# Splitting a scratch write and a broadcast load by their outermost dimension of four

## Chip, cores, metric

One core of a Trainium2 chip. The metric is the time of one execution on the device, in microseconds (us). One run of the kernel before, 1818.09 us, was slow and is in no ratio. The rounds ran on more than one chip, and every ratio is to the kernel before in the same rounds.

## The reference, cut to what matters

```python
# x: (1, 512, 512, 96) bf16; dw: 3x3x96; w1: 96x384; w2: 384x96
out = depthwise_conv3x3(x, dw)
h = layernorm(out)                       # over the 96 channels
h = gelu(h @ w1)
gx = sqrt((h * h).sum(over all pixels) + 1e-6)
nx = gx / (gx.mean(-1) + 1e-6)
return x + (grn_gamma * (h * nx) + grn_beta + h) @ w2
```

`nx` needs a sum over all pixels, so the kernel passes twice over the image. Phase 1 makes the convolution, the norm, the first matmul and the sums. Phase 2 applies `w2`, with `h` either read back ("stored" blocks) or computed again from the normed values `yn` ("recompute" blocks). A block is four image rows; there are 128, and of each ten, three are stored and seven recomputed.

## The kernel before

The convolution leaves y on 128 partitions, partition = 32 x image row (r, 0 to 3) + channel group (c, 0 to 31), with three channels (i) by 512 pixels along the free dimension. The first matmul wants channels on the partitions, so `yn` goes through DRAM: a write, then a read in another shape. The reciprocal deviations (`r_dram`) are broadcast from DRAM to the 32 partitions of each row.

```python
def yn_dst(q):                                   # DRAM side of the write
    return yn_dram[q].rearrange("(c i) (r w) -> r c i w", i=NI, r=GR)     # GR = 4
# ... cut ...
def stage_bcast(k):                              # once for four blocks
    b0, n = BATCHES[k]
    rbc = rbcpool.tile([128, BATCH, W], bf16, name="rbc")
    sp.dma_start(out=rbc[:, :n, :].rearrange("p n w -> p (n w)"),
                 in_=bass.AP(r_dram[b0].tensor, r_dram[b0].offset,
                             [[n * W, GR], [0, 32], [1, n * W]]))         # four rows outermost
# ... cut ...
def stage_write(b):                              # once for each block
    sp.dma_start(out=yn_dst(b), in_=yns.pop(b)[:])
def stage_read(b):
    sp.dma_start(out=yn_ring[b % NYT][:C], in_=yn_src(b))                 # ynT
```

The loop is software-pipelined: a step runs the convolution of block s, the normalization (POOL) of an earlier block, the write and read of blocks between, and the first matmul of block s - 14. In this loop every transfer is issued by one engine, SP.

## Time and profile before

1797.85 us, median of 3 runs (1796.64 to 1807.63). From the profiled execution:

| | phase 1 (400 to 800 us) | phase 2 (1250 to 1795 us) |
|---|---|---|
| PE, ACT, DVE, POOL busy | 84%, 76%, 74%, 75% | 94%, 89%, 51%, 88% |
| mean DMA share | 0.61 | 0.98 |

First the page's strips, 40 slices of the span: the busy tenths of PE, and the mean busy tenths of the 16 DMA engines. The change of phases is the dip near slice 28.

```profile
PE   5588888887888889878888888656999999999998
...
DMA  3455656666565656665666565553999999999996
```

Then the windows view: busy us of each engine (and instructions), the granted clock, the DMA share and GB/s.

```profile
core 0: us, PE busy (x) PEld busy (x) DVE busy (x) ACT busy (x) POOL busy (x), PEclk, DMA share, GB/s
...
400.00:800.00 400.00, 336.38 (x7317) 188.61 (x7378) 295.75 (x486) 302.21 (x304) 301.18 (x224) 0.95 0.61 207
...
1250.00:1795.00 545.00, 511.38 (x7169) 375.62 (x7166) 276.78 (x510) 485.96 (x351) 482.17 (x286) 0.96 0.98 348
```

Phase 2 is full of DMA. Phase 1 shows nothing full, which by itself says only that an average hides the limit. The waits view (who waited for whom: us in total, times, longest) shows DMA behind several engines, first of all behind SP:

```profile
SPq L32 <- DMA yn_dram<-yn: 363.7, 97, 5.7
...
SPq L32 <- DMA r_dram<-rt: 78.2, 35, 3.8
...
SPq L32 <- DVE rt L32: 44.6, 17, 13.4
...
```

```profile
POOL yn L32 <- DMA rbc<-r_dram: 212.6, 31, 14.1
...
PE U L32 <- DMA ynT<-yn_dram: 82.7, 32, 10.1
...
PE Y L32 <- DVE y_bf L32: 35.4, 12, 5.6
```

The chain of work that ended last, from 100 to 1130 us, by line:

```profile
by line: DMA ynT<-yn_dram 14.9%; PE U L32 10.3%; DMA r_dram<-rt 9.4%; DVE bst L32 8.6%; DMA yn_dram<-yn 8.4%; PE Y L32 8.0%; SPq L32 4.8%; issue 4.4%; PE SG L32 4.3%; ACT gm L32 3.8%; ACT gt L32 3.7%; DVE xT L32 3.0%; another core or an unk
```

The DMA view has the number of transfers and the size of each:

```profile
yn_dram<-yn SPq DMA_DIRECT2D x128, 384.0 KB
...
rbc<-r_dram SPq DMA_DIRECT2D x31, 512.0 KB
```

What no view shows is how the 16 DMA engines share the load. The trace has a start and a length for every packet, so I counted the packets in flight at each moment from 100 to 1100 us. The count is of the queue that carries the kernel's own transfers; the fetches of instructions, which have a queue of their own, are left out here and in every such count below (with them, exactly four is 28% and five 17%):

```
packets in flight    0 to 3    exactly 4    5       6 to 14    15 and more
share of the time    0.02      0.36         0.10    0.16       0.36
```

The records don't name the engine of a packet. I read a lasting state of exactly four as four engines at work while the others have nothing to do; e3, e4 and e10 below test this reading.

### The profile page before, as it was taken

The page shows a single profiled execution, that of the slowest core. Times are in us where ns is not written, and L with a number is a line of the kernel's source. Part 1 is how long each engine was busy: PE and PEld are TensorE (multiplying, and loading weights), DVE is VectorE, ACT ScalarE, POOL GpSimd, SP SyncE. Part 2 cuts the span into 40 slices and gives each one's busy share as a digit, 9 for nine tenths or more (in the row PEclk, how much of TensorE's full clock was granted, in tenths as well). Part 3 has the DMA queues.
Part 4 walks back from the last instruction along what each step waited for, and adds up shares of the span by engine and source line. Part 5 has one row for each costly group of instructions (what it writes and reads, how often), then busy time and mean ns, then how long its engine had stood idle before and what let it go on. Part 6 is the DMA issues. An engine that isn't in the chain of part 4 may idle for free.

```text
span 1795.2 us, 63594 instructions
## 1 busy us (share of the span) xinstructions
PE 1508.7 (84%) x28145; PEld 926.2 (52%) x28302; DVE 1147.9 (64%) x1989; ACT 1371.8 (76%) x1236; POOL 1359.9 (76%) x972
## 2 busy tenths in 40 slices
PE   5588888887888889878888888656999999999998
PEld 2254444444444445444444444423667666666666
DVE  4256877777768677867786767656545554455455
ACT  2357777776777678767776778766989898889898
POOL 5678876787678767866787677532999998889896
PEclk9698999999999999999998989887999999999999
DMA  3455656666565656665666565553999999999996
GB/s 95 120 171 175 219 197 210 205 219 210 200 221 201 212 196 221 204 203 200 216 206 207 196 207 178 195 204 115 361 357 367 365 362 337 351 347 367 353 372 261
DMA packets 171879, 430.92 MB, mean 240 GB/s; under 512 B 27796, under 2 KB 77300, under 8 KB 171604
## 3 DMA queue, kind: packets, MB, share of 16 engines
q1 hardware_dynamic: 154212, 357.11, 58.2%
q0 software_dynamic: 15568, 69.74, 11.0%
q8 instruction: 222, 3.64, 0.8%
q14 instruction: 53, 0.43, 0.1%
q10 hardware_dynamic: 1824, 0.00, 0.1%
HBM read 267.41 MB, written 159.38 MB: 238 GB/s over the span
## 4 chain that ended last, share of the span: by engine, by line
DMA 37%; PE 32%; DVE 10%; ACT 9%; issue 4%; POOL 4%; SPq 4%; another core or an unknown queue 2%; ACTq 0%; DVEq 0%; POOLq 0%
PE U L32 15%; DMA ynT<-yn_dram 10%; DMA out_dram<-o_sb 10%; PE O L32 9%; DMA yn_dram<-yn 6%; DMA r_dram<-rt 6%; DVE bst L32 6%; PE Y L32 5%; SPq L32 3%; PE SG L32 3%; ACT gm L32 3%; ACT gt L32 2%; DVE xT L32 2%; ACT gth L32 2%; DMA gl<-g_dram 2%
## 5 line engine op out<-in xcount | busy, mean ns | idle before, releaser
L32 POOL TENSOR_TENSOR yn<-y_bf,rbc 128x1536 bf16<-128x1536 bf16 x128 | 396.5, 3097 | 245.4 <-DMA rbc<-r_dram 212.6
L32 ACT ACTIVATE gl<-U 128x1536 bf16<-128x1536 f32 x356 | 493.1, 1451 | 63.5 <-PE U L32 50.9
L32 DVE TENSOR_TENSOR o_sb<-O,xb 128x384 bf16<-128x384 f32 x512 | 277.8, 556 | 268.3 <-PE O L32 202.6
L32 DVE BATCH_NORM_STATS2 bst<-gth 128x6 f32<-128x512 bf16 x534 | 332.0, 672 | 172.6 <-ACT gth L32 172.6
L32 PE MATMUL Y<-xT,Wd 32*32 32x511 bf16 (+1 forms) x13374 | 359.6, 406 | 85.1 <-DVE y_bf L32 35.4
L678 POOL TENSOR_TENSOR xb<-xr,B2c 128x1536 f32<-128x1536 bf16 x128 | 400.5, 3130 | 26.8 <-DVE o_sb L32 17.6
L32 ACT ACTIVATE gth<-U 128x1024 bf16<-128x1024 f32 x267 | 263.6, 1026 | 203.1 <-issue 141.9
L32 POOL TENSOR_TENSOR ysq<-y_bf 128x1536 bf16<-128x1536 bf16 x128 | 351.6, 2747 | 47.2 <-ACT y_bf L32 23.7
L32 PE MATMUL U<-ynT,w1p 128*128 128x512 bf16 x845 | 285.7, 411 | 120.9 <-DMA ynT<-yn_dram 82.7
L32 PEld LDWEIGHTS <-gl 128*128 128x128 bf16 x6048 | 305.5, 99 | 120.0 <-issue 39.6
L32 DVE BATCH_NORM_STATS2 bst<-gt 128x6 f32<-128x512 bf16 x444 | 269.3, 676 | 128.7 <-ACT gt L32 128.4
L32 PE MATMUL O<-W2s,gl 128*128 128x96 bf16 x6048 | 326.5, 209 | 29.6 <-DVE o_sb L32 28.4
L32 PEld LDWEIGHTS <-w1p 96*128 96x128 bf16 (+1 forms) x2070 | 167.9, 100 | 326.3 <-issue 155.1
L32 PE MATMUL U<-ynl,w1p 96*128 96x512 bf16 x1068 | 300.8, 391 | 7.9 <-DVE junk L32 7.5
L32 PEld LDWEIGHTS <-Wd 32*32 32x32 bf16 x13806 | 165.5, 90 | 271.2 <-issue 212.7
L32 ACT ACTIVATE gt<-U 128x1024 bf16<-128x1024 f32 x222 | 215.4, 1033 | 71.6 <-remote 60.2
L32 ACT ACTIVATE gm<-U 128x1024 bf16<-128x1024 f32 x267 | 263.8, 1033 | 5.0 <-PE U L32 4.8
L32 ACT ACTIVATE y_bf<-Y 128x1536 bf16<-128x1536 f32 x102 | 148.6, 1456 | 45.7 <-PE Y L32 45.6
L32 DVE STREAM_TRANSPOSE xT<-xin 128x576 f32<-128x576 f32 (+1 forms) x256 | 181.0, 747 | 2.3 <-DMA xin<-in_x_dram 2.3
L32 PE MATMUL U<-w1p,ynT 128*128 128x384 bf16 (+2 forms) x1068 | 159.1, 283 | 12.2 <-ACT gth L32 4.2
L32 PEld LDWEIGHTS <-ynT 128*128 128x128 bf16 x1068 | 91.4, 101 | 99.8 <-issue 70.0
L32 PE MATMUL SG<-gm 128*128 128x128 bf16 x2136 | 136.2, 220 | 3.8 <-issue 3.7
(77 smaller groups left out, 731.7 us busy)
## 6 DMA issues: line engine op xcount, KB each, us to landing
g_dram<-gt SPq DMA_DIRECT2D x111, 512.0 KB
xin<-in_x_dram SPq DMA_DIRECT2D x126, 432.0 KB
yn_dram<-yn SPq DMA_DIRECT2D x128, 384.0 KB
ynT<-yn_dram SPq DMA_DIRECT2D x128, 384.0 KB
xr<-in_x_dram POOLq DMA_DIRECT2D x128, 384.0 KB, 7.7
out_dram<-o_sb SPq DMA_DIRECT2D x128, 384.0 KB
gl<-g_dram SPq DMA_DIRECT2D x74, 512.0 KB
ynl<-yn_dram SPq DMA_DIRECT2D x89, 384.0 KB
```

The costliest lines, as they stand in the source:

```text
L32: r = f(*a, **k)
L678: nc.gpsimd.tensor_tensor(out=xb[:], in0=grp[q]["xr"][:], in1=B2c[:, None, :].to_broadcast([128, PXP, C]), op=ALU.add)
```

## The change

The intent is that the outermost dimension of both kinds of transfer is 32 or more, so that each can use all 16 DMA engines.

```diff
-    def yn_dst(q):
-        return yn_dram[q].rearrange("(c i) (r w) -> r c i w", i=NI, r=GR)
+    def yn_dst(q, r):
+        return yn_dram[q].rearrange("(c i) (r w) -> r c i w", i=NI, r=GR)[r]
@@ stage_bcast
-            sp.dma_start(out=rbc[:, :n, :].rearrange("p n w -> p (n w)"),
-                         in_=bass.AP(r_dram[b0].tensor, r_dram[b0].offset, [[n * W, GR], [0, 32], [1, n * W]]))
+            for j in range(GR):
+                sp.dma_start(out=rbc[32 * j:32 * j + 32, :n, :].rearrange("p n w -> p (n w)"),
+                             in_=bass.AP(r_dram[b0].tensor, r_dram[b0].offset + j * n * W, [[0, 32], [1, n * W]]))
@@ stage_write
-            sp.dma_start(out=yn_dst(b), in_=yns.pop(b)[:])
+            yn = yns.pop(b)
+            for r in range(GR):
+                sp.dma_start(out=yn_dst(b, r), in_=yn[32 * r:32 * r + 32, :, :])
```

## The prediction

> **What bounds the kernel now.** Phase 1 (convolution, norm, first matmul) runs to about 1215 us, phase 2 after it. In the windows view, phase 2 (1250 to 1795 us) has the DMA share at 0.98; the change does not touch it. In phase 1 (400 to 800 us) no engine is full: PE 84%, ACT 76%, DVE 74%, POOL 75%, mean DMA share 0.61. The mean hides the limit. I counted packets in flight from the trace's packet records: from 100 to 1100 us exactly four were in flight in 36% of the time, fewer in only 2%. Four engines never rest while twelve often do. The 1,024-byte packets (yn writes) took 2,001 us in that 1,000 us window: 50% of each of four engines. The rbc broadcasts (26 batches of 128 packets of 4 KB, mean 197 ns) add about 16%, everything else, spread over sixteen, about 43%. The sum passes 100%: four engines are full, and phase 1 goes at their pace. The Trainium skill, "DMA: Bandwidth & Descriptors", section "Why a DMA increments its semaphore by 16 and not by 1", says a transfer uses the largest number of engines up to 16 that divides the outermost dimension of both sides: 4 for the yn write and the broadcast. The four in flight agree.
>
> **How it reaches the time.** In the waits view SP waits 364 us for yn writes (97 times), POOL 213 us for rbc, PE 83 us for ynT. In the chain, from 100 to 1130 us, ynT reads have 14.9%, r_dram 9.4%, yn writes 8.4%.
>
> **What the change does.** Bytes, packets and compute stay; the instruction order on PE, ACT, DVE and POOL is the same. yn writes and broadcasts have 32 outermost (96 on the write's DRAM side), so 16 engines each. The load becomes about 60% on all sixteen. Added: 384 + 102 issues on SP, 0.31 to 0.54 us each in the trace: about 1.7 us per step, SP then issuing 3 to 4 us of a step of 8. The issue order shows eight completion semaphores in turn, so a DMA waits for the one eight before it; with nine issues a step that is mostly the previous step's. The broadcast's last parts now wait for a g store and an x load just issued: a few us of SP once in four steps, with two steps of slack behind it. I expect none of this on the critical path.
>
> **Size.** A phase-1 step takes 8.83 us on average (first convolution matmul to the next). Undisturbed steps (lower quartile) are 6.8, 8.0 and 7.9 us by kind (recompute after stored, recompute after recompute, stored after recompute); weighted 0.3/0.4/0.3 that is 7.6, PE without a gap. ACT, DVE and POOL would each be near 90% then, so I allow 0.25 us of hiccups: 7.85. 121 steps times 1.0 us is 120 us, plus about 10 in the ramp, where the first ynT read takes 11 us. Phase 2: unchanged.
>
> Predicted: 1667 us, range 1630 to 1720 (8 in 10). Faster by over 2%: 0.94; within 2%: 0.05; slower by over 2%: 0.01.
>
> **What would show it.** Phase 1's DMA share rising to about 0.67, the four-in-flight plateau gone; SP's wait for yn writes and POOL's for rbc under 60 us each; PE in phase 1 at 93% or more; ynT and r_dram nearly gone from phase 1's chain; phase 2 as long as before (within 1%).
>
> **What would make it wrong.** Steps stay at 8.4 us or more since SP, with its in-order waits on eight semaphores, becomes the limit; DVE and ACT in stored steps lag more than undisturbed steps show; a 32-partition transfer is slower per packet; the granted clock drops as PE fills.

## More of the kernel before

One more part matters later, the copy of y out of PSUM (`y_bf`). PSUM holds one Y, so the next step's convolution waits for this copy:

```python
# per step, in the order of issue on the vector engine (DVE):
squares(...)                    # 12 statistics instructions in a stored step, 6 in a recompute step
turn_x(s + 2)                   # two transposes
evac(pm_rows(b) > 0 and s % 4 == 0)   # True: copy y on DVE, else on ACT; pm_rows > 0: recompute step
```

## The result, and the profile after

1730.42 us, median of 4 runs (1723.24 to 1740.58), against 1800.76 us (4 runs) for the kernel before in the same rounds. The ratio is 0.961, 95% interval 0.9549 to 0.9671. A ratio here is the mean time of one kernel's fast runs over that of the other's of the same rounds, so not quite the ratio of the medians. The gain is clear. It is about half of the predicted one, and the time lies above the predicted range.

The same lines after. Strips, then windows:

```profile
PE   5688888889888989898988998659989899999998
...
DMA  3458557766786578667857766767999999999995
```

```profile
400.00:800.00 400.00, 346.41 (x7542) 193.69 (x7600) 309.62 (x509) 311.44 (x313) 306.17 (x233) 0.95 0.71 219
...
1180.00:1731.00 551.00, 509.24 (x7172) 373.01 (x7170) 276.61 (x512) 485.86 (x351) 483.47 (x286) 0.97 0.97 344
```

The DMA share rose to 0.71, but PE is at 346.41 of 400 us, 87%. Waits of SP, then of the others:

```profile
SPq L32 <- DVE rt L32: 284.9, 33, 14.6
...
SPq L32 <- DMA yn_dram<-yn: 9.7, 9, 2.9
...
SPq L32 <- DMA r_dram<-rt: 1.0, 3, 0.4
```

```profile
PE Y L32 <- DVE y_bf L32: 35.7, 12, 5.6
...
PE Y L32 <- issue: 20.4, 23, 2.1
POOL yn L32 <- DMA rbc<-r_dram: 18.2, 7, 6.3
```

SP now waits for the transposed deviations, that is for the compute engines: it runs ahead of them. PE's wait for ynT is nearly gone:

```profile
PE U L32 <- DMA ynT<-yn_dram: 1.3, 1, 1.3
```

What did not move at all is PE's wait for the copy of y: 12 times, 35.7 us. The chain from 100 to 1070 us, and the transfers:

```profile
by line: PE Y L32 16.4%; PE U L32 16.2%; DVE bst L32 13.4%; PE SG L32 9.6%; issue 9.0%; ACT gm L32 6.8%; ACT gt L32 5.7%; another core or an unknown queue 4.4%; ACT y_bf L32 4.3%; ACT gth L32 3.9%; DVE xT L32 3.6%; DVE y_bf L32 1.9%; DVE mv
```

```profile
yn_dram<-yn SPq DMA_DIRECT2D x512, 96.0 KB
...
rbc<-r_dram SPq DMA_DIRECT2D x124, 128.0 KB
```

No transfer is left in the visible part of phase 1's chain. Exactly four packets were in flight in 0.7% of the time, none in 22%, 15 and more in 52%.

Where the 64 us between the two profiled executions went, from the start times in the traces:

| stretch | before | after | difference |
|---|---|---|---|
| start to first matmul U | 78.6 | 75.0 | -3.6 |
| to the last copy of y (the convolution loop) | 1039.0 | 996.1 | -42.9 |
| to the last U of phase 1 (pipeline drain) | 112.5 | 89.8 | -22.7 |
| the rest, phase 2 with it | 565.1 | 570.3 | +5.2 |

The +5.2 is no effect of the change: a second profile of the changed kernel (e12 below) has 556.7 there. That profile has 983.9 in the loop, so single profiles of one kernel differ by 12 to 14 us in such a stretch.

Setting the steps of the two traces side by side shows what changed and what didn't. Step = from the first convolution matmul to the next step's, in us; the numbering starts at the first convolution after the first statistics matmuls. The columns e2 and e5 are experiments below.

```
step    before   after   e2      e5
 32     15.50    9.00    8.51    8.50      <- waits for ynT in before
 52     12.57    8.51    8.50    8.52
 72     14.84    8.51    8.50    8.50
 92     13.74    8.81    8.51    8.50
112     15.53    8.86    8.51    8.37
 18      9.26    9.26    9.26    6.82      <- a DVE copy right behind a stored step
 26      9.61    9.60    9.61    6.81
 46     12.23   12.25   12.24    6.82
 58     11.89   12.24   11.67    6.84
 66      9.61    9.61    9.60    6.82
```

The first group, five of the steps that waited for ynT in before, lost its DMA waits. The second shows five of eleven such steps, which are within 0.4 us of each other with and without the change; the other six differ by up to 1.0, and all eleven sum to 108.7 us before and 107.4 after.

### The profile page after: what moved, and what is told of

It is laid out like the page before. It is cut to its first block, busy times and chain, and to the rows that moved or that the text cites. A ratio compares the mean times of both kernels' runs of the same rounds, so it can differ in the third digit from the quotient of the medians.

```text
span 1731.2 us, 64436 instructions
## 1 busy us (share of the span) xinstructions
PE 1494.7 (86%) x28145; PEld 919.5 (53%) x28302; DVE 1147.0 (66%) x1989; ACT 1370.4 (79%) x1236; POOL 1362.1 (79%) x972
## 4 chain that ended last, share of the span: by engine, by line
PE 43%; ACT 15%; DMA 15%; DVE 14%; issue 6%; another core or an unknown queue 3%; POOL 2%; SPq 1%; ACTq 0%; DVEq 0%; POOLq 0%
PE U L32 18%; DMA out_dram<-o_sb 11%; PE Y L32 10%; PE O L32 9%; DVE bst L32 9%; PE SG L32 6%; ACT gm L32 5%; ACT gt L32 4%; ACT gth L32 3%; ACT y_bf L32 3%; DVE xT L32 2%; DMA gl<-g_dram 2%; SPq L32 1%; DVE y_bf L32 1%
## 5 line engine op out<-in xcount | busy, mean ns | idle before, releaser
L32 PE MATMUL Y<-xT,Wd 32*32 32x511 bf16 (+1 forms) x13374 | 365.4, 405 | 100.9 <-DVE y_bf L32 35.7
L32 POOL TENSOR_TENSOR yn<-y_bf,rbc 128x1536 bf16<-128x1536 bf16 x128 | 397.0, 3102 | 24.5 <-DMA rbc<-r_dram 18.2
L32 PE MATMUL U<-ynT,w1p 128*128 128x512 bf16 x845 | 275.7, 397 | 41.3 <-ACT gm L32 12.9
L32 PE MATMUL U<-w1p,ynT 128*128 128x384 bf16 (+2 forms) x1068 | 153.5, 275 | 16.0 <-ACT gth L32 6.3
```

The source lines that it names most:

```text
L32: r = f(*a, **k)
```

## The experiments

Twelve more runs were made, eleven kernels and a repeat, all of them with correct results. The first question was whether four full DMA engines were the cause; the second, where the rest of the forecast gain is.

**e1: only the yn writes split.** The broadcast stays as it was.

```diff
-            for j in range(GR):
-                sp.dma_start(out=rbc[32 * j:32 * j + 32, ...   # the four parts
+            sp.dma_start(out=rbc[:, :n, :] ...                 # one transfer, as before
```

> Only the yn writes are split; the broadcast stays one transfer on four engines. Theory A (four full engines were the limit of phase 1): by the loads counted in the trace of before, the four engines carry about 12% (yn spread over sixteen) + 16% (rbc on four) + 43% = 71%, no longer full, so nearly the whole gain of the full change appears: ratio to before 0.960 to 0.970, and POOL's wait for rbc falls below 60 us though the broadcast is untouched. Rival B (POOL's 213 us wait for rbc, the longest wait at a compute engine, was the limit by itself): little gain here, ratio 0.99 or more, and POOL still waits for rbc.

Measured: 1719.87 us, ratio 0.9561 (0.9512 to 0.9611). The whole gain, even a little more than expected. But POOL's wait for rbc did not fall below 60 us:

```profile
POOL yn L32 <- DMA rbc<-r_dram: 102.2, 25, 10.4
```

So that detail of the expectation was wrong, and the wait is largely harmless: POOL waits 102 us for rbc in a kernel as fast as the full change. The largest wait of a compute engine in before was no measure of what removing it would give.

**e2: only the broadcasts split.** The yn writes stay one transfer with r = 4 outermost.

> Only the broadcasts are split; the yn writes stay on four engines. Theory A: the four engines still carry 50% + 4% + 43% = 97% and stay the limit: ratio 0.985 to 1.0, exactly four packets in flight still in over 20% of phase 1, SP still waits 200 us or more for yn writes. Rival B (the broadcast was the limit): ratio 0.960 to 0.970.

Measured: 1725.5 us, ratio 0.9558 (0.9498 to 0.9618). This is again the whole gain, and theory A as written (0.985 to 1.0) missed. Its other two expectations held: exactly four in flight in 20.5% of the time, and SP still waits for the writes.

```profile
SPq L32 <- DMA yn_dram<-yn: 332.9, 95, 5.7
```

Rival B gets its number here, but e1 had already shown that the broadcast can be left alone. What failed is my sum of loads. Before added up to 109%, which can't be: an engine has more than one packet in flight at times (in before, 17 and more were in flight on 16 engines in 12% of the time). If 109% stands for "full at 8.83 us a step", then 97% stands for 97/109 x 8.83 = 7.9 us, less than the 8.2 to 8.4 us that a step takes in e2 and in after. This was worked out after the fact; e8 below was to test it. In the time, either half of the change gives the whole gain.

**e3: the write in three transfers by i.** More and smaller transfers, all still with r = 4 outermost.

```diff
-            sp.dma_start(out=yn_dst(b), in_=yns.pop(b)[:])
+            yn = yns.pop(b)
+            for i in range(NI):
+                sp.dma_start(out=yn_dst(b)[:, :, i, :], in_=yn[:, i, :])
```

> The yn write is split into three transfers by i, each with r = 4 outermost and all 128 partitions: more and smaller transfers, but still four engines. Theory A: as before, ratio 0.99 to 1.015, four in flight still in a third of phase 1. Rival C (the gain came from smaller transfers, which are more of them in flight and land earlier, not from more engines): most of the gain, ratio 0.96 to 0.975.

Measured: 1797.73 us, ratio 0.9976 (0.9932 to 1.0019), exactly four in flight in 37% of the time. Rival C is out: splitting as such gives nothing. A trap is in this run's waits. SP's wait for the writes fell too, and the time didn't:

```profile
SPq L32 <- DMA yn_dram<-yn: 58.9, 74, 4.4
```

```profile
PE U L32 <- DMA ynT<-yn_dram: 71.1, 25, 10.1
```

**e4: the write in two transfers, two rows each.** Now two is outermost.

```diff
+            for r in range(0, GR, 2):
+                sp.dma_start(out=yn_dst(b)[r:r + 2], in_=yn[32 * r:32 * r + 64, :, :])
```

> The yn write as two transfers of two rows each, so two is outermost; broadcast as before. Theory A: two engines carry 100% (yn) + 16% + 43% = about 1.6 of the time that before needs for it, against 1.09 in before, so phase 1 (1,130 us) grows by about 46%: about 2,300 us in all, and the packet records show two in flight for over half of phase 1. Rival C (more transfers in flight is what helps): no slower than before.

Measured: 2307.76 us, ratio 1.281 (2 runs; 1.2734 to 1.2886), with exactly two packets in flight in 41% of the time and three in 11% (expected: two in over half). The forecast of 2,300 put two engines in place of four into the same sum of loads that e2 shows to be off, so its closeness is partly luck (phase 1 to its last U grew by a factor of 1.41, not 1.46). The direction and the plateau at two are not luck: with e3, they show that the number of engines counts, and not the number of transfers:

```profile
PE U L32 <- DMA ynT<-yn_dram: 531.1, 124, 13.3
```

The Trainium skill, "DMA: Bandwidth & Descriptors", section "Why a DMA increments its semaphore by 16 and not by 1", gives the rule by which the outermost dimension sets the number of engines; the counts here (four in flight for four, two for two, no plateau for 32) agree.

**e5: the full change, with the vector engine's copies of y moved.** In 11 steps the DVE copy comes right behind a stored step, whose twelve statistics instructions are still queued on DVE. This part of the timeline of the changed kernel shows one: start us, length, and in brackets the idle time before and what ended it.

```profile
537.68 0.44 PE L32 MATMUL SG<-rowsel,ysq 128*128 128x4 bf16 x12
543.69 1.50 PE L32 MATMUL Y<-xT,Wd 32*32 32x512 bf16 x36 [5.57 <-DVE y_bf L32]
```

```profile
530.85 4.80 DVE L32 BATCH_NORM_STATS2 bst<-gt 128x6 f32<-128x512 bf16 x8
535.58 2.76 DVE L32 BATCH_NORM_AGGREGATE mv<-bst 128x2 f32<-128x192 f32 x3
538.26 1.22 DVE L32 BATCH_NORM_STATS2 bst<-gth 128x6 f32<-128x512 bf16 x2
539.39 1.42 DVE L32 STREAM_TRANSPOSE xT<-xin 128x576 f32<-128x576 f32 x2
540.74 1.24 DVE L32 BATCH_NORM_STATS2 bst<-gth 128x6 f32<-128x512 bf16 x2
541.90 1.74 DVE L32 CAST y_bf<-Y 128x1536 bf16<-128x1536 f32 x1
```

PE is idle for 5.57 us until the copy (CAST) at 541.90 is done, and the copy stands behind 11 us of other work, nearly all statistics, with no gap on DVE. The next burst of 36 convolution matmuls takes 1.50 us; a burst elsewhere in this trace takes 0.89. The records of the granted clock have 0.5 from 542.4 us on, for 6.8 us. The Trainium skill, "TensorE: Matmul & The Clock Gate", section "Why this matters for your kernels", warns that idle gaps of PE above about 3 us bring the half clock; this gap of 5.57 us did. (This step, number 58, is one of the two slowest of the eleven.)

```diff
-                    evac(pm_rows(b) > 0 and s % 4 == 0)
+                    evac(pm_rows(b) > 0 and pm_rows(b - 1) > 0 and s % 2 == 0)
```

> The full change, and the copies of y out of PSUM that run on the vector engine are moved to recompute steps that follow a recompute step (about as many, 23 for 22). In before and in the changed kernel the same 11 steps, those with such a copy right behind a stored step, take 9.3 to 12.3 us, since the copy stands behind twelve statistics instructions and PE waits for it (36 us, 12 times, in all traces so far). Theory D (what the forecast counted as DMA trouble is this compute wait, which the change cannot touch): PE's wait for the copy falls below 10 us, and the time falls 25 to 50 us below the changed kernel's: ratio to before 0.935 to 0.948. Rival E (the copy's wait is slack that another engine takes over, the loop is limited by the engines' sum): ratio 0.955 or more.

Measured: 1692.09 us, ratio 0.9388 (0.9346 to 0.9431). PE's wait for DVE's copy is all but gone:

```profile
PE Y L32 <- DVE y_bf L32: 0.4, 1, 0.4
```

All eleven steps of that kind are at 6.8 us (column e5 above), and theory D holds. (The recorded 9.3 to 12.3 us is too narrow: in after the eleven steps take 8.5 to 12.3.) Over the eleven steps alone the traces of after and e5 differ by 32 us.

**e6: all copies on ACT.**

```diff
+                    evac(False)
```

> The full change, and all copies of y out of PSUM on ACT. Theory D: PE's wait for DVE's copy is gone altogether; ACT gets 22 x 1.3 us = 29 us more work and stays under 95%, so ratio to before 0.935 to 0.955. Rival E: ratio 0.96 or more.

Measured: 1699.81 us, ratio 0.9445 (0.9402 to 0.9488), as theory D expected.

**e7: the same move of the copies in the kernel before.**

> The kernel before, with the same move of the copies and no split. Theory A and D together: four full engines still set phase 1's pace, so the 36 us that PE no longer waits for the copy come back as waits for ynT: ratio 0.985 to 1.0. If the two losses are separate and simply add, ratio 0.975 to 0.98.

Measured: 1800.04 us, ratio 1.0004 (0.9961 to 1.0047). The same edit that gives 1.7 to 2.2% behind the change gives nothing without it. PE no longer waits for the copy and waits for ynT instead, 112.6 us in place of 82.7:

```profile
PE U L32 <- DMA ynT<-yn_dram: 112.6, 42, 10.3
```

**e8: only the broadcasts split, and the copies moved.**

> Only the broadcasts split, with the same move of the copies. The four engines' load is 97% of what 109% cost before: about 7.9 us a step, under the changed kernel's 8.4 but about what e5 should need. Theory A and D: the four engines come back as a limit, ratio 0.942 to 0.955, at most 0.01 above e5. If four engines no longer matter once the broadcast is split: the same as e5 within 0.004.

Measured: 1700.08 us, ratio 0.9441 (0.9403 to 0.9478). The interval overlaps that of e5, so whether the four engines cost anything here is not decided by the time. The trace leans to yes: exactly four in flight in 21.5% of the time, and PE waits 27.5 us for ynT, against 4.2 us in e5.

**e9: only the writes split, and the copies moved.**

> Only the yn writes split, broadcast on four engines, copies of y moved as in e5. The four engines carry 71% of what is 109% at the pace of before, so they are no limit at 7.9 us a step either: ratio to before 0.930 to 0.945, the same as e5 within 0.008, with 102 fewer transfers.

Measured: 1690.75 us, ratio 0.9366 (0.9329 to 0.9403): as e5, without the 102 extra transfers.

**e10: no split, another layout of the scratch tensor.**

```diff
-    yn_dram = dram.tile([NBLK, C, GR * W], bf16, name="yn_dram")
+    yn_dram = dram.tile([NBLK, 128, NI * W], bf16, name="yn_dram")
-        return yn_dram[q].rearrange("c (r w) -> c r w", r=GR)
+        return yn_dram[q].rearrange("(r c) (i w) -> (c i) r w", r=GR, i=NI)
-        return yn_dram[q].rearrange("(c i) (r w) -> r c i w", i=NI, r=GR)
+        return yn_dram[q]
```

> No split at all: the scratch tensor in DRAM is laid out as the yn tile lies in on-chip memory (128 rows of 3 KB), so one yn write has 128 outermost and 16 engines; reads of it then come as 1 KB packets in place of 4 KB. Broadcast on four engines, copies of y moved as in e5. If the number of engines is what counts, and not the number of transfers: as e9, plus at most 15 us in phase 2 for the smaller packets of the re-reads (89 x 384 packets of 47 ns against 89 x 96 of 159 to 197 ns, over 16 engines): ratio 0.930 to 0.955. If splitting as such is needed: 0.98 or more.

Measured: 1744.25 us, ratio 0.965 (0.9611 to 0.9689), between the two expectations. The kernel to compare it with is e7, which has the same copies and no split either: 1.0004. So one transfer on 16 engines gains 3.5% without any splitting, and it relieves the four (exactly four in flight: 6.6% against 36%). But it stays behind e9. Phase 2 from its 200th output matmul on took 546 us against 535 in e9; the 15 us allowed for the 1 KB re-reads would cover that, but the other profiles, whose phase 2 is unaltered, spread from 522 to 539 us. Phase 1 up to its last U took 43 us more than in e9 (1162.8 against 1119.9), which nobody expected; the trace puts 24 us of it into idle time of PE without a semaphore behind it (43.8 us from 100 to 1000 us, against 19.4 in e9). The rest is in PE's busy time: in the convolution loop it is 874 us against 854 in e9, with 59 us at the half clock against 20. Why the layout brings these gaps is open.

**e11: e5, with the Gram products spread out.** PE has gaps with no semaphore behind them ("issue" in the waits), more of them the faster phase 1 goes. In the traces of before, after, e5 and e10 together there are 74 of them over 0.5 us between 100 and 1040 us, and every one ends 1.24 to 1.63 us after a packet of 16 KB on the instruction queue has landed. In e5 such packets land 148 times in these 940 us, so a moment picked at random has that distance about once in sixteen (148 x 0.39 / 940). By their number these packets are PE's: the page of before counts 222 of them on that queue, and PE has 28,145 matmuls and 28,302 weight loads, 254 for each. So I take it that PE was waiting for its own instructions. The Trainium skill, "Runtime: NRT & Kernel Launch", section "Instruction fetch mechanics", describes refills in blocks of 256 instructions (16 KiB) and calls their cost "mostly hidden"; here it is not always.

```diff
                 us[3]()
+                for f in grams[:1]:
+                    f()
@@
                 us[4]()
+                for f in grams[1:]:
+                    f()
                 us[5]()
@@
-                for f in grams:
-                    f()
```

> e5, with the two halves of the Gram products (24 weight loads and 24 matmuls each) moved from the end of the step to between the expansion matmuls, so that the stretch of short PE instructions around a step's end is less dense. Same work, same results. Theory F (the idle time of PE that e5 still has, 33 us with no semaphore behind it, is PE waiting for instructions, because 16 KB fetches of them come too slowly for dense stretches): those gaps fall below 17 us and the time falls 8 to 25 us below e5: ratio 0.925 to 0.935. Rival: the gaps have another cause, stay at 25 us or more, and the time stays within 0.005 of e5.

Measured: 1667.57 us, ratio 0.9243 (0.9206 to 0.9279), a little better than theory F expected and apart from e5's interval. But the gaps fell only from 33 to 24 us (100 to 1000 us), not below 17. So at most 9 of some 25 us gained can be put down to them. Even that is doubtful: PE's idle time in the whole convolution loop is 94 us here and 92 in e5, and what fell is its busy time (853 us against 876, but e9 without this edit has 854 too). Theory F is not shown as the reason, and where the 25 us come from is open. It is the fastest version tried, 7.6% under the kernel before.

**e12: the full change again.**

> The full change once more, unaltered, on this chip, as the comparison for e9 to e11 and as a second profile of it: ratio 0.955 to 0.967; PE waits for the vector engine's copy of y 12 times, 34 to 37 us; gaps of PE without a semaphore 10 to 30 us.

Measured: 1726.91 us, ratio 0.9554 (0.9509 to 0.9599). The two measurements of the same kernel, 0.961 and 0.9554, show how finely e1, e2 and the full change can be told apart: not at all. In this profile PE waits for the copy 11 times, 34.0 us (100 to 1000 us), and the gaps without a semaphore sum to 16.3 us, against 24.7 in the first profile of the same kernel. They vary by run, and so does the time.

## Why the prediction was right and wrong

- **Four full DMA engines bounded phase 1: right.** e3 (more transfers, four engines: 0.9976), e4 (two engines: 1.281), e10 against e7 (one transfer on 16 engines: 0.965 against 1.0004) and e1, e2 (either load taken off: 0.956) show it. The sum of loads behind it was not right: 109% can't be, and with it e2 was forecast as no gain. The plateau of four went from 36% to 0.7%.
- **What the change adds is off the critical path: right in effect, too small in size.** I expected 0.31 to 0.54 us of SP for each added issue. In the timeline of after, a group of four write issues takes 2.7 to 3.5 us, about 0.7 to 0.9 each, waits between them included. It cost nothing that can be seen, since SP then waits 285 us for compute.
- **SP's wait for the writes and POOL's for rbc under 60 us: right** (9.7 and 18.2). **Chain without ynT and r_dram: right. Phase 2 as long as before: right** (565.1 and 570.3 us from the last U on). **DMA share about 0.67: 0.71.** Packets took longer than in before (1,024-byte packets 50 ns in place of 47, 4,096-byte ones 215 in place of 197), and there are 9,726 more, nearly all under 512 bytes, where the forecast had "packets stay".
- **PE at 93% or more: wrong** (87%).
- **The failing step is the paragraph "Size".** "Undisturbed steps (lower quartile)" were taken as what every step becomes, with "0.25 us of hiccups". A lower quartile leaves out everything that disturbs a step, DMA or not. One third of one kind of step (the 11 copies behind stored steps, 8.5 to 12.3 us in place of 6.8) was slow for a reason that the change can't touch, and the page had it in plain sight as 35 us of PE waiting for `y_bf`. The steps went to 8.44 and 8.31 us (the two profiles) in place of 7.85. The forecast allowed 121 x 0.25 = 30 us of hiccups in all; in the loop of after, PE has 85 us of gaps over 0.15 us: 36 for the copy, 30 without a semaphore (14 in before, so part of the gain was lost again there), 19 for ACT and the transposes. The loop gave 43 us (55 in e12's profile) in place of "120", the ramp 4 in place of "about 10", and the pipeline's drain, which I had not counted at all, 23.
- **The list of what would make it wrong** had this failure in it: "DVE and ACT in stored steps lag more than undisturbed steps show". It also had steps of 8.4 us or more, but with SP as the reason; SP's 285 us of waiting for compute speak against that. The granted clock did not drop: 0.95 from 400 to 800 us in both.
- **What takes the rest, as far as shown.** Moving the copies gives 0.9388 against 0.961 and 0.9554 for the change alone: 30 to 40 us of the 63 that were missing (1730 - 1667). Spreading the Gram products gives about 25 more. Its 1667.57 us equals the forecast by luck, since the forecast had neither edit in it, and the cause of this second part is open.

A simpler sum from the same trace would have come out closer. PE is the engine that phase 1 turns into its limit, and its idle time for `ynT` was 82.7 us; the measured gain was 70. A second pair agrees: in e7 PE waits 112.6 us for `ynT`, and e5, the same kernel with the split, is 108 us faster. Both sums were made after the fact.

## What to carry to other kernels

A mean DMA share well under one doesn't clear DMA: count the packets in flight, and look at the outermost dimension of each transfer, since a few engines can be full while the rest idle. To size the gain of removing a limit, take the idle time that this limit causes on the next engine in line, cause by cause (it came out 18% too high here and 4% too high in e7 and e5); don't compare with the best steps, which are free of every other trouble too. And an edit that gave nothing behind a limit (e7) is worth trying again once the limit is gone (e5).

## What the Trainium skill lacked or had wrong

- "DMA: Bandwidth & Descriptors", section "Rules for kernel authors": for two transfers to disjoint partition halves it says "Don't bother", and to use one 128-partition transfer. It lacks the exception: with a leading dimension of four on the DRAM side, one 128-partition write was slower than four 32-partition ones (e1, the four: ratio 0.9561 to before, the one). The row there on using all 16 engines names the remedy, but not this conflict.
- No page says how to see an uneven load of the DMA engines in packet records that don't name the engine, as here ("Perfetto Trace Analysis" has tracks for each engine). Here a mean share of 0.61 went with four full engines; the count of packets in flight (exactly four in 36% of the time) showed it.
- "Runtime: NRT & Kernel Launch", section "Instruction fetch mechanics", calls the cost of a refill mostly hidden. 74 gaps of PE over 0.5 us end 1.24 to 1.63 us after a 16 KB instruction packet landed; from 8 us in total in before to 41 us in e10, 0.9% and 4.4% of the 940 us looked at. "Mostly" holds, but in e5's loop they are the largest cause of PE's idle time, 35 us.
